# The last MoE phase of a fused attention and two-MoE kernel: the second MoE's first two token pairs woven into it, its last four output operands converted in place

## The chip, the cores and the metric

One NeuronCore of a Trainium2 chip runs the whole program. The metric is the device time of one execution in microseconds. The engines run side by side, each through its own queue in program order: TensorE (PE in the rows, with PEld for its weight loads), VectorE (DVE), ScalarE (ACT), GpSimd (POOL), and SyncE (SP), which issues most transfers.

## The reference

```python
out = softmax(q @ k.T / 8) @ v              # chunks of 64 positions, 8 heads, 4608 tokens
x   = (h := out @ w_in) * clip(h + 3, 0, 6) / 6 @ w_out      # first MoE, 512 -> 2048 -> 512
h   = x @ w_in2                              # second MoE, 512 -> 1024
s   = h * softmax(h)
out = ((s - mean(s)) / sqrt(var(s) + 1e-6) * g_ln) @ w_out2  # 1024 -> 512
```

All data are float32. The kernel keeps float32 precision by splitting each operand into a rounded high part and the low rest, and by adding up three of the four products.

## The kernel before, in words

Tokens are handled in 9 blocks of 512 in the first MoE. Blocks 3 to 8 are handled as three pairs of blocks. The function `pair` computes one pair in two phases. The **first phase** runs over 16 chunk pairs `j` and computes the hidden layer with seven block products per `j` (a Strassen-Winograd scheme), gates half of the results and parks the other half in DRAM (`held`). The **second phase** (steps `i` = 0 to 15) loads the parked results, gates them (ACT a relu, DVE a multiply), splits them (ACT a cast to `g_hi`, DVE a subtraction to `g_lo`) and multiplies them with `w_out`: one call of `moe_o` is 12 matmuls into the banks `acc`, and the call for step `i` stands on TensorE two steps later, before that step's other work. After the last call, the four `acc` banks are moved out (L548, L550) and stored to `x2d`.

The second MoE works on 18 pairs of 128-token tiles. For a pair `p`, `fetch_x2` loads its tokens, `combine_x2` forms four sums on DVE, `split_x2` makes the high parts on ACT and the low parts (`x_lo`). `product_1` to `product_7` are seven products of six matmuls each, into three banks `a`, `b` and `c`, of which `sum_2`, `sums_7`, `product_3` and `product_4` form the two hidden tiles on DVE. Each tile `t` then goes through `soft_1` (DVE row maximum, ACT exponential), `soft_2` (DVE), `turn` (DVE transposes inside blocks of 32, then block moves: by DMA from SP, by POOL in `pool_moves`, by ACT in `rest_moves`, eight copies), `chain_square` and `chain_rstd` (variance), `split_l` (the split for the last product), and `out_mm` (24 matmuls into a bank `po`). The main loop over `p` lays the work out so that the outputs on TensorE lag two pairs behind the products.

The weights of the second MoE are prepared while the last pair's first phase runs: the class `Second` reads them, forms the combined operands, splits them, and stores them to DRAM (`st2`); `load_2` brings them back in the second phase, when SBUF space has come free. `end_work(i)` is called at the end of each step `i` of the last second phase. It issues these loads and the preparation of pair 0, and from the table `EARLY` its products, in steps 11 to 15.

The order on every engine is the order of the code (`manual_schedule`); the pools only add the waits for buffers. A line that matters for what follows:

```python
        if at == NF - 1:
            for dc in range(KD):
                ...
                if dc % 2 == 0:
                    nc.scalar.mul(out=xo, in_=acc[dc], mul=1.0 / 6.0)
```

Of the kernel before, what the change touches and what calls it, by code (L numbers as in the profile page):

```python
# [16 lines left out]
P = 128  # L17
# [4 lines left out]
def tile_kernel(  # L22
# [168 lines left out]
    class Second:  # L191

        def __init__(self):
            w = wide("kbd")
            self.free = [w[:, i] for i in range(2)]
# [27 lines left out]
        def scale(self):  # L223
            if self.chunks and self.scaled != self.chunks[0]:
                self.scaled = self.chunks[0]
                r = self.raw[self.chunks[0]][:, :, 1]
                nc.scalar.activation(out=r, in_=r, func=AF.Copy, scale=2.0**-112)

# [37 lines left out]
        def step(self):  # L266
# [18 lines left out]
        def hi(self):  # L285
            for item in self.small:
                if len(self.halves) == 2 or not self.places:
                    break
                if item[0] == "lo" and item[1] in self.w and not self.ready(item):
                    i, w = self.places.pop(0), self.w[item[1]]  # L290
                    if i == 3:
                        t = [wcp.tile([P, DM], F32R, tag=f"{n}3", name=n) for n in ("s", "xo")]
                    else:
                        t = wide("pbd", F32R) if i == 2 else wi_slot(NF - 2 + i, F32R)
                        t = pair_of(t)
# [20 lines left out]
    LOADS = [n for n, (o, j) in enumerate(OPERANDS) if o[0] == "B" or o == "T1"]  # L316
    LOADS += [n for n in range(len(OPERANDS)) if n not in LOADS]

    def load_2(n):

        name, j = OPERANDS[n]
        homes = {"B11": 0, "T1": 1, "B21": 2, "B22": 3}
        if name == "out":
            t = wi[KD * NS + j] = wi_slot(KD * NS + j, F32R)
        elif name in homes:
            t = wi_slot(4 * j + homes[name], F32R)
            w2[name, j] = pair_of(t)
        elif j == 0 and name in ("T2", "T3"):
            t = wide({"T2": "kbd", "T3": "pbd"}[name], F32R)
            w2[name, j] = pair_of(t)  # L330
        else:
            t = None
            w2[name, j] = {
                ("T4", 0): lambda: (narrow(ap2, "v"), narrow(ap2, "v")),
                ("T2", 1): lambda: (narrow(ap2, "p"), narrow(ap2, "p")),
                ("T3", 1): lambda: (narrow(ap1, "q"), narrow(ap1, "tx0")),
                ("T4", 1): lambda: (narrow(ap1, "tx1"), narrow(ap1, "tx2")),
            }[name, j]()
        if t is None:
            for i in range(2):  # L340
                nc.sync.dma_start(out=w2[name, j][i].bitcast(F32), in_=st2[n][:, i])
        else:
            nc.sync.dma_start(out=t.bitcast(F32), in_=st2[n])
# [184 lines left out]
    def moe_o(b, f, g, at=None):  # L528
# [105 lines left out]
    def fetch_x2(p):  # L634
        if p < NU // 2:
            if p == 1:
                xr2[p] = [wo_slot(4 + i, F32).rearrange("p c (j t) -> p (c j) t", t=P) for i in range(2)]
            else:
                xr2[p] = [xrp.tile([P, 8, P], F32, tag=f"xr{i}", name=f"xr{i}") for i in range(2)]
# [55 lines left out]
    def bank(p, tag):  # L695

        if p:
            c_t[p, tag] = ps_2.tile([P, DM], F32, tag=tag, name=tag)
        else:
            if not early:  # L700
                early.append(att_psum())
            c_t[p, tag] = h_psum() if tag == "c" else early[0][:, int(tag == "b")]
        return c_t[p, tag]

    early = []

    def part(p, n):
        c_t[p, n] = work_tile("xo" if n == "s1" and not p else "s", name=n)
        return c_t[p, n]
# [66 lines left out]
    def turn(t):  # L776
# [3 lines left out]
        m = ring(8, 2, t).rearrange("p (b x) -> p b x", b=4)  # L780
# [48 lines left out]
    def l_tiles(i):  # L829

        if i < 3:
            return [
                (wo_slot(10 + 2 * i + k, F32R).rearrange("p c (f t) -> p (c f) t", t=P),)
# [41 lines left out]
    def out_mm(t):  # L875
# [3 lines left out]
        for a, ws in ((l_hi, (0, 1)), (l_lo, (0,))):  # L879
            for f in range(NF2):  # L880
                for w in ws:
                    nc.tensor.matmul(  # L882
                        po, a[f], wi[KD * NS + f][:, w],
# [232 lines left out]
    def pair(p, todo):  # L1116
# [6 lines left out]
        for j in range(NJ):  # L1123
# [37 lines left out]
            mul7(a, j, "A12", "B21", False, True)  # L1161
            if fill:
# [12 lines left out]
            mul7(c, j, "S4", "B22", False, True)  # L1175
            c12 = work_tile("xo")
# [42 lines left out]
        if final:  # L1219
            flush()  # L1220
            for n in LOADS[-3:]:
                load_2(n)
        return todo

    def end_work(i):
        m = len(OPERANDS) - NF2
        for n in LOADS[m * i // 11 : m * (i + 1) // 11] if i < 11 else LOADS[m + i - 11 :][:1]:
            load_2(n)
        if i == 0:
            fetch_x2(0)  # L1230
        elif i == 4:
            combine_x2(0)
        elif i == 5:
            split_x2_hi(0)
            split_x2_lo(0, 0, nc.vector)
        elif i == 6:
            split_x2_lo(0, 1, nc.vector)
            fetch_x2(2)
        elif i == 7:
            fetch_x2(1)  # L1240
        elif i == 9:
            combine_x2(1)
        elif i == 10:
            split_x2_hi(1)
            split_x2_lo(1, 0, nc.vector)
        elif i == 11:
            split_x2_lo(1, 1, nc.vector)
        for step in EARLY.get(i, ()):
            step(0)


    EARLY = {
        11: (product_1,),
        12: (product_6, product_2),
        13: (product_5, product_7, sums_7),
        14: (product_4,),
        15: (product_3,),
    }
# [85 lines left out]
    product_1(1)  # L1344
    soft_1(1)
    product_6(1)
    sum_2(1)
    combine_x2(2)
    split_x2(2)
    fetch_x2(3)  # L1350
    soft_1(0)
    product_2(1)
    product_7(1)
    product_5(1)
    sums_7(1)
    soft_2(1)
    turn(1)
    product_4(1)
    product_3(1)
    product_1(2)  # L1360
    product_6(2)
    sum_2(2)
    pool_moves(1)
    rest_moves(1)
    soft_2(0)
    product_2(2, False)
    product_7(2)
    product_5(2)
    chain_square(1)
    sums_7(2)  # L1370
    turn(0)
    split_l_hi(1)
    chain_square(0)
    keep_2(2)
    pool_moves(0)
    rest_moves(0)
    split_l_lo(1)
    soft_1(3)
    combine_x2(3)
    product_4(2)  # L1380
    product_3(2)
    split_l(0)
    split_x2(3)
    soft_1(2)
    chain_rstd(0)
    out_next()
    soft_2(3)
    fetch_x2(4)
    turn(3)
    square(3)  # L1390
    out_next()
    product_1(3)
    soft_1(5)
    soft_2(2)
    product_6(3)
    sum_2(3)
    turn(2)
    chain_square(2)
    split_l(3)
    stores()  # L1400
    pool_moves(2)
    rest_moves(2)
    combine_x2(4)
    soft_1(4)
    product_5(3)
    product_2(3)
    soft_2(5)
    split_x2(4)
    split_l(2)
    chain_rstd(1)  # L1410
    for p in range(3, NP):
        last = 2 * p - 2
        if p > 3:
            product_1(p)
            stores()
            split_l(last - 2)
            product_6(p)
            product_5(p)
            sum_2(p)
            turn(last + 1)  # L1420
            square(last + 1)
            product_2(p)
            soft_2(last)
            product_7(p)
# [102 lines left out]
```

## Time and profile before

| what | value |
|---|---|
| runs before | 1226.52, 1226.36, 1223.59 us; median 1226.36 us |
| the profiled execution | 1226.5 us, of which the span of the instructions is 1224.7 us |
| TensorE busy | 1190.7 us, 97% of the span |
| VectorE, ScalarE, GpSimd busy | 952.3, 656.9 and 381.8 us |
| mean granted TensorE clock | 0.993 |

TensorE's busy time is that of overlapping matmuls; a matmul of 512 columns shows some 390 ns, and a new one begins every 227 ns when nothing is in the way. Times in the trace count from the first instruction. The last second phase starts at 792.5 us, the second MoE's own part (after `es.close()`) at 852.5 us.

### The profile page before, as it was taken

The page shows a single profiled execution, that of the slowest core. Times are in us where ns is not written, and L with a number is a line of the kernel's source. Part 1 is how long each engine was busy: PE and PEld are TensorE (multiplying, and loading weights), DVE is VectorE, ACT ScalarE, POOL GpSimd, SP SyncE. Part 2 cuts the span into 40 slices and gives each one's busy share as a digit, 9 for nine tenths or more (in the row PEclk, how much of TensorE's full clock was granted, in tenths as well). Part 3 has the DMA queues.
Part 4 walks back from the last instruction along what each step waited for, and adds up shares of the span by engine and source line. Part 5 has one row for each costly group of instructions (what it writes and reads, how often), then busy time and mean ns, then how long its engine had stood idle before and what let it go on. Part 6 is the DMA issues. An engine that isn't in the chain of part 4 may idle for free.

```text
span 1224.7 us, 20699 instructions
## 1 busy us (share of the span) xinstructions
PE 1190.7 (97%) x7268; PEld 970.7 (79%) x7268; DVE 952.3 (78%) x1754; ACT 656.9 (54%) x1353; POOL 381.8 (31%) x466
## 2 busy tenths in 40 slices
PE   6899999999999999999999999999989999999998
PEld 5677788878788888888888888887768888888887
DVE  7999687787677779777778777774997878878774
ACT  4676455453322237322246343363788777877775
POOL 3000243530011110011100112100676767665865
PEclk9999999999999999999999999999999999999999
DMA  9800584441355537355445798794222323232311
GB/s 369 362 26 27 210 304 132 159 152 61 104 198 207 194 108 249 108 189 190 175 138 201 264 335 291 252 377 174 86 68 90 99 71 99 72 97 69 100 54 63
DMA packets 110360, 199.82 MB, mean 163 GB/s; under 512 B 14000, under 2 KB 49072, under 8 KB 107184
## 3 DMA queue, kind: packets, MB, share of 16 engines
q1 hardware_dynamic: 103920, 186.97, 44.1%
q10 hardware_dynamic: 6336, 11.54, 2.5%
q8 instruction: 57, 0.93, 0.3%
q14 instruction: 47, 0.39, 0.1%
HBM read 129.50 MB, written 58.20 MB: 153 GB/s over the span
## 4 chain that ended last, share of the span: by engine, by line
PE 83%; DVE 11%; ACT 2%; issue 1%; DMA 1%; SPq 1%; POOL 1%; DVEq 0%; ACTq 0%; POOLq 0%
PE acc L537 28%; PE po L882 14%; PE hp L1040 14%; PE hp L498 7%; PE att L1040 5%; PE b L684 5%; PE c L684 3%; PE a L684 3%; PE att L386 3%; DVE s L171 2%; DVE g_lo L523 1%; SPq L797 1%; DVE s L163 1%; DVE pbd L460 1%; PE att L684 1%
## 5 line engine op out<-in xcount | busy, mean ns | idle before, releaser
L537 PE MATMUL acc<-g_hi,wo 128*128 128x512 f32 x1152 | 294.9, 393 | 1.4 <-ACT g_hi L520 1.3
L537 PEld LDWEIGHTS acc<-g_hi,wo 128*128 128x128 f32 x1152 | 215.4, 189 | 48.8 <-DVE xo L550 1.9
L523 POOL TENSOR_TENSOR g_lo<-t,g_hi 128x512 fp32r<-128x512 f32 x45 | 65.6, 1457 | 450.8 <-ACT g_hi L520 450.8
L537 PE MATMUL acc<-g_lo,wo 128*128 128x512 f32 x576 | 160.0, 389 | 1.3 <-DVE g_lo L523 1.3
L882 PE MATMUL po<-wi,wo 128*128 128x512 f32 x648 | 152.5, 392 | 1.3 <-ACT ob L891 1.3
L882 PEld LDWEIGHTS po<-wi,wo 128*128 128x128 f32 x648 | 122.6, 189 | 27.5 <-ACT ob L891 1.7
L1040 PE MATMUL hp<-wi,ws 128*128 128x512 f32 x576 | 142.7, 390 | 0.0
L460 DVE STREAM_TRANSPOSE pbd<-p 32x128 f32<-32x128 f32 x448 | 135.5, 303 | 6.7
L537 PEld LDWEIGHTS acc<-g_lo,wo 128*128 128x128 f32 x576 | 108.2, 188 | 24.3 <-DVE g_lo L523 1.7
L1040 PEld LDWEIGHTS hp<-wi,ws 128*128 128x128 f32 x576 | 107.9, 188 | 23.7 <-DVE s L1146 1.2
L665 POOL TENSOR_TENSOR x_lo<-xr,x_hi 128x768 fp32r<-128x768 f32 (+1 forms) x32 | 70.3, 2218 | 135.0 <-DVE xr L651 64.0
L797 ACT COPY wo<-wo 32x256 f32<-32x256 f32 x228 | 92.0, 404 | 17.4 <-DVE wo L779 11.3
L498 PE MATMUL hp<-x_hi,wi 128*128 128x512 f32 x384 | 97.9, 397 | 2.0 <-ACT wi L352 1.9
L520 ACT CAST g_hi<-t 128x512 fp32r<-128x512 f32 x112 | 69.4, 620 | 53.0 <-DVE t L513 36.0
L498 PEld LDWEIGHTS hp<-x_hi,wi 128*128 128x128 f32 x384 | 72.5, 191 | 18.9 <-ACT wi L352 2.7
L1106 ACT ACTIVATE t<-att,three 128x512 f32<-128x512 f32 x24 | 16.5, 688 | 130.4 <-PE att L1040 113.8
L769 DVE SCALAR_TENSOR_TENSOR wo<-wo,r,wo 128x1024 f32<-128x1024 f32 x36 | 77.4, 2151 | 1.3
L1011 POOL TENSOR_TENSOR xo<-tx,xo 128x512 fp32r<-128x512 f32 x16 | 20.8, 1320 | 181.7 <-ACT xo L1005 167.0
L1040 PE MATMUL att<-wi,wa 128*128 128x512 f32 x288 | 73.1, 389 | 0.0
L866 POOL TENSOR_TENSOR wo<-wo,wo 128x1024 fp32r<-128x1024 f32 x26 | 63.4, 2439 | 6.8 <-ACT wo L862 3.3
L1040 PEld LDWEIGHTS att<-wi,wa 128*128 128x128 f32 x288 | 54.1, 188 | 11.3
L504 ACT ACTIVATE t<-hp,three 128x512 f32<-128x512 f32 x48 | 33.1, 691 | 50.4 <-PE hp L498 50.4
(269 smaller groups left out, 2194.6 us busy)
## 6 DMA issues: line engine op xcount, KB each, us to landing
ws<-sts SPq DMA_DIRECT2D x24, 1024.0 KB, 6.7
wa<-stw SPq DMA_DIRECT2D x24, 512.0 KB, 4.0
held<-xo SPq DMA_DIRECT2D x42, 256.0 KB, 2.2
s<-held SPq DMA_DIRECT2D x42, 256.0 KB, 4.4
wo<-wo SPq DMA_DIRECT2D x328, 32.0 KB, 1.8
x2d<-xo SPq DMA_DIRECT2D x36, 256.0 KB, 3.0
out<-ob SPq DMA_DIRECT2D x36, 256.0 KB, 2.2
v<-in_v SPq DMA_DIRECT2D x34, 256.0 KB, 2.7
```

Source lines behind the costliest of these rows:

```text
L460: nc.vector.transpose(out=pb[o : o + 32, s // 2, s % 2], in_=pv[s * 32 : s * 32 + 32, c, e],)
L498: nc.tensor.matmul(hp, wi[f][:, a, kk * P : (kk + 1) * P], b[:, kk], start=(n == 0), stop=(n == 3 * KD - 1),)
L520: nc.scalar.copy(out=g_hi, in_=t)
L523: eng.tensor_sub(out=g_lo, in0=t, in1=g_hi.bitcast(F32))
L537: nc.tensor.matmul(acc[dc], wo[f][:, w, dc * P : (dc + 1) * P], g[i], start=(at == 0 and n == 0), stop=(at == NF - 1 and n == 2),)
L665: eng.tensor_sub(out=lo[:, f], in0=r, in1=hi[:, f].bitcast(F32))
L684: nc.tensor.matmul(ps, x[:, AT[a], j], w2[w, j][i], start=(start and n == 0), stop=(stop and n == 5), skip_group_check=True,)
L769: nc.vector.scalar_tensor_tensor(out=h, in0=e, scalar=r, in1=h, op0=ALU.mult, op1=ALU.mult, accum_out=mu)
L797: move(out=m[b * 32 : b * 32 + 32, a], in_=tr[a * 32 : a * 32 + 32, b])
L866: eng.tensor_sub(out=lo, in0=m, in1=hi.bitcast(F32))
L882: nc.tensor.matmul(po, a[f], wi[KD * NS + f][:, w], start=(n == 0), stop=(n == 3 * NF2 - 1),)
L1040: nc.tensor.matmul(ps, w[:, i, kk * P : (kk + 1) * P], x[:, kk], start=(start and n == 0), stop=(stop and n == 5), skip_group_check=True,)
```

## The change

- Pairs 0 and 1 of the second MoE are both computed inside the steps of the last second phase: products of pair 0 in steps 3 to 8, those of pair 1 in steps 9 to 14, and between them the soft-max, the turning and the splits of their tiles as far as they are ready. The code after `es.close()` that did pairs 1 and 2 by hand is gone; the main loop begins at `p = 2`.
- `load_2` begins in the last chunk pair of the first phase (eight loads, and the first tokens of pair 0), and each operand takes the slots of the first phase's operand of the same name.
- The last four output operands are not stored to `st2` and loaded again: `place` gives them a home in SBUF, and `out_w` keeps them there. Four output operands are still loaded, in steps 9, 11, 13 and 15.
- Slots are renumbered (`ring(14, ...)`, `l_tiles`), pairs 0 and 1 share one PSUM tile for `a` and `b`, and the move of the `acc` banks goes ACT, ACT, DVE, DVE in place of turn about.

The core of the diff:

```diff
+        def place(self, kept):
+            if kept and all(any(t is w for t in self.free) for w in self.wide):
+                if len(self.free) > 2 or not self.chunks:
+                    self.free = [t for t in self.free if all(t is not w for w in self.wide)]
+                    self.wide = [None]
+                    return None, pair_of(wide("kbd", F32R))
...
+            i = min(self.places) if kept else max(self.places)
...
-                self.to_store.append((name, t, i))
+                if i is not None:
+                    self.to_store.append((name, t, i))
...
+                    kept = o == "out" and n >= LOADED_OUT
+                    i, t = self.place(kept)
...
+                    if kept:
+                        out_w[n] = t
...
+    LOADED_OUT = 4
+    out_w = {}
+    LOADS = [(n, j) for n in ("B11", "T2", "T1", "B21", "T3", "T4", "B22") for j in range(NS)]
+    LOADS += [("out", i) for i in range(LOADED_OUT)]
...
         else:
+            t = wi_slot(2 * XQ.index(o) + j, F32R)
+            w2[o, j] = pair_of(t)
+            nc.sync.dma_start(out=t.bitcast(F32), in_=st2[OPERANDS.index((o, j))])
...
-                if dc % 2 == 0:
+                if dc < 2:
                     nc.scalar.mul(out=xo, in_=acc[dc], mul=1.0 / 6.0)
...
-        if p:
+        if p > 1:
             c_t[p, tag] = ps_2.tile([P, DM], F32, tag=tag, name=tag)
         else:
+            if p not in early:
+                early[p] = att_psum()
+            c_t[p, tag] = h_psum() if tag == "c" else early[p][:, int(tag == "b")]
...
-        m = ring(8, 2, t).rearrange("p (b x) -> p b x", b=4)
+        m = ring(14, 2, t).rearrange("p (b x) -> p b x", b=4)
...
             mul7(a, j, "A12", "B21", False, True)
+            if final and lastj:
+                for n in range(4):
+                    load_2(n)
+                fetch_x2(0)
...
             mul7(c, j, "S4", "B22", False, True)
+            if final and lastj:
+                for n in range(4, 8):
+                    load_2(n)
...
     def end_work(i):
+        if 8 + i < len(LOADS) - LOADED_OUT:
+            load_2(8 + i)
+        elif i in (9, 11, 13, 15):
+            load_2(len(LOADS) - LOADED_OUT + (i - 9) // 2)
+        for step, *a in EARLY[i]:
+            step(*a)
...
+    EARLY = [
+        [],
+        [(combine_x2, 0)],
...
+        [(product_7, 1), (sums_7, 1), (turn, 1), (chain_square, 1)],
+        [(product_4, 1), (soft_2, 0), (split_x2_lo, 2, 0, nc.vector), (pool_moves, 1), (rest_moves, 1)],
...
-    product_1(1)
-    soft_1(1)
...
+    rest_moves(0)
     product_1(2)
+    chain_rstd(0)
     soft_1(2)
-    chain_rstd(0)
...
+    for p in range(2, NP):
...
+        if p == 2:
+            soft_2(3)
```

How it moves instructions is seen at three places. On TensorE, at the end of the last second phase, before (`acc` is a `moe_o` call, `hp` the last product of pair 0, `a` the first product of pair 1):

```order
L684 MATMUL hp<-wi_8299,x_lo 128x512
L537 MATMUL acc_8176<-g_hi,wo_1159 128x512 x2
L537 MATMUL acc_8177<-g_hi,wo_1159 128x512 x2
...
L537 MATMUL acc_8177<-g_hi,wo_1250 128x512 x2
L537 MATMUL acc_8177<-g_lo,wo_1250 128x512
L684 MATMUL a<-wi_8132,x_hi 128x512 x2
```

And of the change at the same place, where the `hp` row is the last product of pair 1 and `a`, `b` are the first products of pair 2:

```order
L689 MATMUL hp<-wi_8304,x_lo 128x512
L545 MATMUL acc_8188<-g_hi,wo_1105 128x512 x2
...
L545 MATMUL acc_8189<-g_hi,wo_1250 128x512 x2
L545 MATMUL acc_8189<-g_lo,wo_1250 128x512
L689 MATMUL a<-wi_8053,x_hi 128x512 x2
```

So 42 matmuls of pair 1 have moved from behind the phase into it, and three `moe_o` calls stand between them and pair 2. On VectorE, in the last steps of that phase, before (L513 is the gate, L523 `g_lo`, L742 to L753 are sums of pair 0, L550 the move out of `acc`, L758 the first row maximum of any tile):

```order
L513 SCALAR_TENSOR_TENSOR t<-t,s 128x512
L523 TENSOR_TENSOR g_lo<-t,g_hi 128x512
L748 TENSOR_TENSOR wo_8529<-s_8454,att 128x512
L523 TENSOR_TENSOR g_lo<-t,g_hi 128x512
L753 TENSOR_TENSOR wo_8491<-u_8483,hp 128x512
L550 TENSOR_SCALAR xo<-acc_8176 128x512
L550 TENSOR_SCALAR xo<-acc_8177 128x512
L758 TENSOR_REDUCE nmx<-wo_8529 128x1
```

And of the change, steps 13 to 15 (L753 and L758 are now the sums of pair 1's `product_4` and `product_3`, L771 to L778 `soft_2` of tile 0, L784 its `turn`, L871 the low part of `split_l` of tile 1, L521 and L531 the gate and `g_lo`):

```order
L753 TENSOR_TENSOR wo_8576<-s_8459,att 128x512
...
L774 SCALAR_TENSOR_TENSOR wo_8312,mu<-wo_8492,r,wo_8312 128x1024
L777 TENSOR_SCALAR mu<-mu 128x1
L778 TENSOR_SCALAR wo_8312<-wo_8312,mu 128x1024
L670 TENSOR_TENSOR x_lo<-xr_8418,x_hi 128x768
L521 SCALAR_TENSOR_TENSOR t<-t,s 128x512
L531 TENSOR_TENSOR g_lo<-t,g_hi 128x512
L758 TENSOR_TENSOR wo_8530<-u_8488,hp 128x512
L784 STREAM_TRANSPOSE wo_8663<-wo_8312 128x1024
L871 TENSOR_TENSOR wo_8671<-wo_8580,wo_8670 128x1024
L531 TENSOR_TENSOR g_lo<-t,g_hi 128x512
```

The gates and low parts that feed `moe_o` now stand behind whole rows of 1024 elements. On SP, at the end of the first phase, before (`held` are the parked results, `st` the stored operands, `x2d` the tokens):

```order
L1183 DMA held<-xo 128x512
L1112 DMA s<-held 128x512 x3
L343 DMA wi_8132<-st 128x1024
L644 DMA xr_8134<-x2d 128x4x128 x2
L551 DMA x2d<-xo 128x512 x4
```

And of the change:

```order
L1195 DMA held<-xo 128x512
L351 DMA wi_8053<-st 128x1024
...
L649 DMA xr_8061<-x2d 128x4x128 x2
...
L351 DMA wi_8105<-st 128x1024
L1117 DMA s<-held 128x512 x3
L351 DMA wi_8144<-st 128x1024
L559 DMA x2d<-xo 128x512 x4
```

Eight operand loads and the tokens now stand ahead of the first three loads of parked results.

## Rows read from the trace of the kernel before

**Rows 1.** The page: span, and busy time of each engine.

```profile
span 1224.7 us, 20699 instructions
PE 1190.7 (97%) x7268; PEld 970.7 (79%) x7268; DVE 952.3 (78%) x1754; ACT 656.9 (54%) x1353; POOL 381.8 (31%) x466
```

**Rows 2.** Stretches: PE, PEld, DVE, ACT, POOL busy (instructions); granted clock, DMA share, GB/s.

```profile
798.00:852.30 54.30, 53.49 (x235) 43.87 (x235) 30.65 (x49) 24.57 (x37) 0.00 (x0) 1.00 0.73 272
852.30:925.50 73.20, 67.37 (x277) 51.97 (x277) 67.97 (x100) 59.02 (x115) 45.95 (x63) 0.98 0.30 96
925.50:1220.80 295.30, 295.30 (x1304) 244.32 (x1302) 227.08 (x342) 219.98 (x405) 198.81 (x283) 1.00 0.26 80
...
920.00:925.50 5.50, 5.50 (x22) 4.47 (x21) 4.98 (x8) 5.33 (x14) 3.25 (x4) 0.83 0.21 61
...
800.00:835.00 35.00, 34.22 (x151) 27.99 (x150) 22.99 (x38) 19.66 (x29) 0.00 (x0) 1.00 1.04 387
```

**Rows 3.** Chain of waits that ended last: start, duration, what.

```profile
787.11 2.72 PE acc L537 x12
...
798.07 27.53 PE acc L537 x120
...
852.51 1.36 PE a L684 x6
...
925.75 1.36 PE b L684 x6
...
928.47 5.44 PE po L882 x24
...
1220.96 0.69 ACT ob L891
```

**Rows 4.** Timeline of TensorE: matmuls that waited longest after 852 us.

```profile
893.43 5.74 PE L882 MATMUL po<-wi,wo 128*128 128x512 f32 x24 [1.29 <-ACT ob L891]
...
917.05 0.73 PE L684 MATMUL b<-pbd,x_hi 128*128 128x512 f32 x2 [2.00 <-DVE u L723]
```

**Rows 5.** Timeline of VectorE: second phase, and one tile in the main loop.

```profile
807.28 0.42 DVE L649 TENSOR_TENSOR xr<-xr 128x256 f32<-128x256 f32 x1
...
808.74 0.68 DVE L513 SCALAR_TENSOR_TENSOR t<-t,s 128x512 f32<-128x512 f32 x1
809.39 0.69 DVE L523 TENSOR_TENSOR g_lo<-t,g_hi 128x512 fp32r<-128x512 f32 x1
810.00 0.95 DVE L665 TENSOR_TENSOR x_lo<-xr,x_hi 128x768 fp32r<-128x768 f32 x1
...
979.31 0.11 DVE L766 TENSOR_SCALAR r<-r 128x1 f32<-128x1 f32 x1
...
981.84 0.68 DVE L742 TENSOR_TENSOR u<-s,b 128x512 f32<-128x512 f32 x1
...
983.16 1.24 DVE L779 STREAM_TRANSPOSE wo<-wo 128x1024 f32<-128x1024 f32 x1
```

**Rows 6.** Lines L769 and L773 of `soft_2`: least, median and greatest duration, ns.

```profile
L769 DVE SCALAR_TENSOR_TENSOR wo<-wo,r,wo x36: 1284/2225/3422, 860.3 to 1201.1; 128x1024 f32<-128x1024 f32 x36
...
L773 DVE TENSOR_SCALAR wo<-wo,mu x36: 752/754/2579, 862.9 to 1204.1; 128x1024 f32<-128x1024 f32 x36
```

**Rows 7.** Groups after 852 us: busy us and mean ns, then idle before.

```profile
L758 DVE TENSOR_REDUCE nmx<-wo 128x1 f32<-128x1024 f32 x36 | 42.2, 1208 | 0.0
...
L797 ACT COPY wo<-wo 32x256 f32<-32x256 f32 x228 | 92.0, 404 | 17.4 <-DVE wo L779 11.3 <-DVE r L766 2.0 <-POOL g_lo L866 0.8
L761 ACT ACTIVATE wo<-wo,nmx 128x1024 f32<-128x1024 f32 x36 | 41.5, 1154 | 18.2 <-DVE nmx L758 18.1
...
L714 ACT COPY s<-a 128x512 f32<-128x512 f32 x17 | 10.0, 587 | 36.9 <-PE a L684 36.8
```

**Rows 8.** Loads of stored operands (L343), and the first relu on a parked result.

```profile
DMA to landing us min/median/max: 4.5/7.1/8.2
...
798.57 0.71 ACT L1106 ACTIVATE t<-s,three 128x512 f32<-128x512 f32 x1
```

More of the change, by code (lines that the diff above doesn't have):

```diff
@@ L194, in __init__ @@
             w = wide("kbd")
-            self.free = [w[:, i] for i in range(2)]
+            self.wide = [w[:, i] for i in range(2)]
+            self.free = list(self.wide)
             self.free.append(ap1.tile([P, DM], F32, tag="q", name="q"))
@@ L227, in scale @@
                 nc.scalar.activation(out=r, in_=r, func=AF.Copy, scale=2.0**-112)
+        def place(self, kept):
[4 more added lines that the diff above has]
+                    return None, pair_of(wide("kbd", F32R))
+            if not self.places:
+                return None, None
+            i = min(self.places) if kept else max(self.places)
+            if kept and i == 3:
+                return None, None
+            self.places.remove(i)
+            if i == 3:
+                return i, [wcp.tile([P, DM], F32R, tag=f"{n}3", name=n) for n in ("s", "xo")]
+            return None if kept else i, pair_of(wide("pbd", F32R) if i == 2 else wi_slot(NF - 2 + i, F32R))
         def words(self):
@@ L635, in fetch_x2 @@
         if p < NU // 2:
[L636 to L639, printed above, removed]
+            xr2[p] = [xrp.tile([P, 8, P], F32, tag=f"xr{i}", name=f"xr{i}") for i in range(2)]
             xr2[p] = [x.rearrange("p (n j) t -> p n j t", j=2) for x in xr2[p]]
@@ L1220, in pair @@
             flush()
-            for n in LOADS[-3:]:
-                load_2(n)
         return todo
     def end_work(i):
[L1226 to L1258, printed above, removed]
+        if 8 + i < len(LOADS) - LOADED_OUT:
[7 more added lines that the diff above has]
+        [(combine_x2, 0)],
+        [(split_x2_hi, 0), (split_x2_lo, 0, 0, nc.vector)],
+        [(split_x2_lo, 0, 1, nc.vector), (fetch_x2, 1), (product_1, 0)],
+        [(product_6, 0), (sum_2, 0)],
+        [(product_2, 0), (product_5, 0), (combine_x2, 1)],
+        [(product_7, 0), (sums_7, 0), (split_x2_hi, 1), (split_x2_lo, 1, 0, nc.vector)],
+        [(product_4, 0), (split_x2_lo, 1, 1, nc.vector)],
+        [(product_3, 0), (fetch_x2, 2)],
+        [(soft_1, 1), (product_1, 1)],
+        [(product_6, 1), (sum_2, 1), (soft_1, 0), (combine_x2, 2)],
+        [(product_2, 1), (product_5, 1), (soft_2, 1), (split_x2_hi, 2)],
+        [(product_7, 1), (sums_7, 1), (turn, 1), (chain_square, 1)],
+        [(product_4, 1), (soft_2, 0), (split_x2_lo, 2, 0, nc.vector), (pool_moves, 1), (rest_moves, 1)],
+        [(product_3, 1), (turn, 0), (split_l, 1, nc.vector), (chain_square, 0)],
+        [(soft_1, 3), (split_x2_lo, 2, 1, nc.vector), (pool_moves, 0), (fetch_x2, 3)],
+    ]
     pend = []
@@ L1368, in tile_kernel @@
[L1368 to L1383, printed above, removed]
-    soft_1(2)
-    chain_rstd(0)
[L1386 to L1411, printed above, removed]
+    rest_moves(0)
+    product_1(2)
+    chain_rstd(0)
+    soft_1(2)
+    for p in range(2, NP):
         last = 2 * p - 2
-        if p > 3:
+        if p > 2:
             product_1(p)
[L1415 to L1424, printed above, removed]
-            sums_7(p)
-            turn(last)
-        else:
-            turn(last + 1)
-            square(last + 1)
-            product_7(p)
-            sums_7(p)
-            soft_2(last)
-            turn(last)
-            fetch_x2(5)
+        stores()
+        split_l(last - 2)
+        product_6(p)
+        product_5(p)
+        sum_2(p)
+        if p == 2:
+            soft_2(3)
+        turn(last + 1)
+        square(last + 1)
+        product_2(p)
+        soft_2(last)
+        product_7(p)
+        sums_7(p)
+        turn(last)
@@ L1435, in tile_kernel @@
         out_next()
         square(last)
-        if p > 3:
-            next_x(p + 1)
+        next_x(p + 1)
         split_l(last + 1)
@@ L1442, in tile_kernel @@
         product_3(p)
-        if p > 3:
-            stores()
+        stores()
         out_next()
```

73 lines of the change are left out of this document (14 added, 59 removed).

## The prediction

> **What bounds the kernel now.** The page comes first: TensorE is busy 97% of the span, no other engine over 78% [rows 1]. So time can only come from the places where TensorE stands still, and these have to be found. The chain of waits gives the pace: 24 matmuls in 5.44 us, 0.2267 us each [rows 3]. From the first `moe_o` call of the last second phase (798.07) to the end of the last output (1220.96) the program has 16 calls of 12, 18 pairs of 42 and 36 output tiles of 24, that is 1812 matmuls, worth 410.7 us; the stretch took 422.9, so 12.2 us are lost in it. The chain says where. Until pair 1 begins (852.51) stand 234 matmuls, worth 53.0 in 54.4: 1.4 lost. From there to 925.75 stand 276 (pairs 1 and 2, then two outputs, pair 3 and two more outputs, mixed), worth 62.6 in 73.2: 10.7 lost. After that 1302, worth 295.1 in 295.2: nothing lost. The view of busy time by stretch shows the same: in 852 to 925 TensorE falls to 67 of 73 us while VectorE is at 68 of 73; afterwards TensorE has no gap at all and VectorE is at 77% [rows 2]. The timeline of TensorE says what ended the waits: an output bank not yet moved out, a sum on VectorE [rows 4]. These are the start of a pipeline: the first tile has to go through maximum, exponential, `soft_2`, turn, moves and split, and there is too little other matmul work to cover that. Meanwhile VectorE stands at 30.7 of 54.3 us and POOL at nothing in 798 to 852 [rows 2]. Part of the 10.7 is clock: 0.83 was granted in 920 to 925.5, between the levels of 1.2 and 2.4 GHz, right after the wait of 2.0 us at 915 to 917 [rows 2, 4].
>
> **The change part by part.** The matmuls stay the same in number; 42 of pair 1 (9.5 us) move into the second phase. Without a stall that phase then runs 798.07 + 16 x 2.72 + 14 x 1.36 = 860.6, with pair 0's products in 803 to 827, pair 1's in 829 to 852.5 and three `moe_o` calls behind them. The first outputs then lie 6.8 us and some 15 us behind 860.6, and the loop has its steady order from the start. So the whole 12.2 us can go, and what is left is what the woven phase and the first section of the loop newly wait for.
>
> VectorE in steps 9 to 15 is the first suspect. Counted from start to start, a gate is 0.65, a low part or sum of 512 columns 0.61, the four sums of `combine_x2` 1.46, `x_lo` 0.95 for 768 columns [rows 5], the maximum 1.21 [rows 7], the turn 1.24 and `soft_2` 2.53 with POOL at rest (979.31 to 981.84) [rows 5]. Each step has one gate and one low part (1.26). Step 10 (sum, maximum, four sums) makes 4.5, step 11 (`soft_2`) 3.8, step 12 (two sums, turn) 3.7, step 13 (sum, `soft_2`, `x_lo`) 5.4, step 14 (sum, turn, low part of `split_l`, by columns 1.27) 4.4: 21.8 against 21.8 us of matmuls in these steps. VectorE is as full as TensorE there, but what it makes is not due at once: the low part of step i is read by the call that stands two steps later, 4.1 us or more behind.
>
> The tightest point is therefore worked through. `product_4` of pair 1 ends at 848.4. From then VectorE runs without a break: sum 0.61, `soft_2` 2.53, `x_lo` 0.95, gate and low part 14 1.26, sum 0.61, turn 1.24, `split_l` 1.27, low part 15 0.61; that ends at 857.5. The call that reads it begins at 857.9 and needs it for its third matmul, 858.4. Cover 0.9 us; each hand-over between engines can eat some of it: 0 to 1.0 us of stall.
>
> Next ScalarE. The maximum of tile 3 ends at 858.7, its exponential (1.15 and 0.19 for the read-out, estimate 1.3) at 860.0, then two moves out of `acc` (0.59 each, by the copy of the same size) 861.2, then tile 0's eight `rest_moves` at 0.404 each, 864.4, then the copy `s1` of pair 2, 865.0 [rows 7]. `product_2` of pair 2 may overwrite nothing before that and is due at 860.6 + 3 x 1.36 = 864.7. Stall 0.3, with what comes late from VectorE up to 1.3.
>
> Third, `product_4` of pair 2, due at 873.2 behind the first output. VectorE: `u2` 865.6, `soft_2` of tile 3 868.1, turn 869.4, `soft_2` of tile 2 871.9, `u3` 872.5. Cover 0.7, if `soft_2` runs at its least. But now POOL works too (`split_l` of tile 0 from about 867), and the two large operations of `soft_2` range from 1.28 to 3.42 and from 0.75 to 2.58 [rows 6]. One blocked L773 makes it 1.1 late: 0 to 1.1.
>
> On that spread the Trainium skill ("SBUF — State Buffer", Who interferes with whom) says that VectorE and GpSimd share a port pair under an exclusive lock: a VectorE operation with two SBUF inputs or in a two-port mode waits out a GpSimd operation that reads SBUF. The rows agree: least in the trace where POOL rests, up to 2.1 us more elsewhere. By that rule the third point is late by 1.1 us or more, by the least durations not at all; I take the middle in the sum below.
>
> The other parts go together at nothing. The eight 256 KB stores and loads that the kept operands save, and the conversions in the first phase, lie beside matmuls that do not wait; VectorE's operations there are the same in number. The earlier loads relieve 800 to 835, where the DMA engines were full (share 1.04, 387 GB/s) [rows 2]; the wait there is part of the 1.4. The new order of moves out of `acc` (ACT, ACT, DVE, DVE) frees the first bank pair after two ScalarE copies of 0.59 in a row in place of 0.6 and 0.69 side by side, and banks come ready 0.68 apart: between -0.1 and +0.1 at each of six block ends.
>
> On SP, everything behind the eight early loads is later: the first three loads of parked results. The last two of the eight wait for the products with B21, which end at 787.1 [rows 3]; the first relu on a parked result ran at 798.6, and stored operands took 4.5 to 8.2 us to land [rows 8]. 787.1 + 1 of issue + 8.2 = 796.3: covered by 2 us, cost 0.
>
> Sum: -12.2, and +0.3 to +3.4 of new stalls, of which I take 2.0 (0.5, 0.7 and 0.8): -10.2 against the profiled execution's own 1226.5 us (span 1224.7 and 1.8 around it), which is 0.1 above the median of the runs: **1216 us**.
>
> **The rivals.**
> - A, as above: the start of the second MoE hides in the phase. For it: VectorE half idle there and POOL free. By the bounds of the stalls, -11.9 to -8.8, and 1.5 us for the spread of the runs, 1213 to 1219.
> - B, VectorE becomes the bound in steps 10 to 15: its 21.8 us of work leave nothing for the waits on products and on ScalarE's exponentials, which stand in the same queue as the relus. Each step of 4.1 us that loses 0.8 to 1.3 to such a wait pushes TensorE; over five or six steps and the first section of the loop, where POOL blocks `soft_2`, 4 to 8 us come back: 1219 to 1223. Against it: the calls lag two steps.
> - C, it does not do what it says: the start is only moved. The first section of the loop (tiles 2 and 3, maximum to split) is again without cover, and waits of 0.8 to 2.0 as in rows 4 return there for some 8 to 12 us: 1223 to 1227. Against it: two outputs of 5.44 us now stand in that section.
> - D, slower: SP. If the eight loads and the tokens (4.7 MB) landed one behind the other at 7.1 us, the first parked result would come after 840, not before 798, and TensorE would stand for 40 us: 1256. It decides from the point where the first parked result lands later than 798.6 + 10.2, where the gain is gone; every further microsecond costs one. Needed is a rate under some 250 GB/s from the first load (about 779) on; 387 were moved in 800 to 835 [rows 2].
>
> The Trainium skill ("TensorE: Matmul & The Clock Gate", What's actually happening) has the low clock as the default that activity lifts; B's waits could then cost clock too, as the one of 2.0 us did, which would put B at its upper end.
>
> **How the numbers follow.** A 0.62, B 0.22, C 0.10, D 0.06. The forecast is A's. The range takes A and nearly all of B: 1212.5 to 1222.5. About 0.3% (3.7 us) is what a measurement here can tell from no change, so faster means below 1222.7: A and nine tenths of B, 0.82; the rest of B and nearly all of C are the same, 0.12; D, 0.06.
>
> **What would show it.** In the trace after: the phase's last call ends at 861 to 863 and the whole part from there on takes 1536 matmuls' worth, 348.2 us, with 1 to 3 us more. Right for the first suspect: TensorE's waits behind 844 stay under 1 us each, and any is on `g_lo` of step 15. Right for the second and third: short waits of the products of pair 2 on the copy `s1` and on `u3`. B shows as TensorE waiting on sums or `g_lo` in several steps from 833 on; C as waits between 861 and 900 like those of rows 4; D as the relus waiting for loads at 797 to 805. The granted clock of 850 to 900 at 1.00 goes with A. The prediction fails most easily where I took least durations on a full VectorE: a few tenths in each of its waits add up, because after step 12 it has no idle time to catch up.

## The result and the profile after

The changed kernel ran in 1214.07 us (median of 6, 1212.95 to 1215.15) beside 1226.44 for the kernel before on the same chip: a ratio of 0.9901 with a 95% interval of 0.9887 to 0.9916, 12.1 us. Two later series gave 0.9908 and 0.9910. The profiled execution took 1213.9 us with a span of 1212.2, against 1224.7 [rows 1].

The page after has the span and the busy times:

```profile
span 1212.2 us, 20680 instructions
PE 1184.8 (98%) x7268; PEld 968.8 (80%) x7268; DVE 948.3 (78%) x1757; ACT 655.9 (54%) x1353; POOL 375.8 (31%) x463
```

The matmuls are as many as before; TensorE stands still less. The timeline of TensorE says where; these are the starts of the first `moe_o` call of the last second phase, of pair 2's first product, and of the last matmul (start, duration, what):

```profile
794.24 0.69 PE L545 MATMUL acc<-g_hi,wo 128*128 128x512 f32 x2
...
857.12 1.07 PE L689 MATMUL a<-wi,x_hi 128*128 128x512 f32 x4
...
1208.10 0.39 PE L887 MATMUL po<-kbd,g_lo 128*128 128x512 f32 x1
```

Before, the first of them stood at 798.07 [rows 3], and the last matmul started at 1220.49 (the last eight began at 1218.90, 0.2267 us apart). So the 12.5 us between the two spans have two parts. **3.8 us** lie ahead of the last second phase, in work that the new order of the second MoE does not touch. **8.5 us** lie in the part that the prediction speaks of: from the first `moe_o` call to the last matmul's start it took 422.4 us and now takes 413.9; 1811 matmuls of 0.2267 us are 410.5, so of 11.9 us lost 3.4 are left. (The prediction's 12.2 counts to the last move out, one matmul and 0.2 us later.) I call this length the stage below. In the three profiled executions of the changed kernel it repeats within 0.1 us, while whole times scatter by some 3 us.

The view of busy time by stretch (as rows 2) says where the 3.4 are: 0.3 up to 857.12 (276 matmuls are 62.6 us), 3.1 from there to 892.97, where TensorE falls to 33.7 of 35.9, nothing after that. The last line is the stretch in which the DMA engines were full before [rows 2]:

```profile
794.24:857.12 62.88, 62.88 (x278) 51.73 (x278) 48.59 (x77) 35.73 (x60) 6.59 (x12) 1.00 0.47 156
857.12:892.97 35.85, 33.69 (x146) 26.93 (x145) 30.40 (x46) 29.38 (x60) 18.86 (x31) 1.00 0.32 102
892.97:1208.50 315.53, 315.52 (x1392) 260.91 (x1391) 244.03 (x371) 236.75 (x437) 213.39 (x301) 1.00 0.26 81
800.00:835.00 35.00, 35.00 (x156) 28.94 (x155) 23.12 (x36) 16.06 (x26) 0.00 (x0) 1.00 0.60 200
```

Only two matmuls behind 848 us still wait for longer than 0.2 us by the timeline of TensorE (in brackets the wait and what ended it), in place of the list from which rows 4 come:

```profile
870.95 1.19 PE L689 MATMUL b<-wi,x_hi 128*128 128x512 f32 x4 [1.20 <-DVE u L747]
...
885.87 1.19 PE L689 MATMUL b<-wi,x_hi 128*128 128x512 f32 x4 [0.97 <-DVE u L728]
```

And this is where the 3.8 us between these two executions come from. Long before the last phase, at the end of a block of the first MoE, TensorE waited for ScalarE. The kernel before, timelines of ScalarE, VectorE and TensorE (two moves out of `acc`, two casts of weight sums, two moves, a waiting matmul):

```profile
229.91 1.09 ACT L548 ACTIVATE xo<-acc 128x512 f32<-128x512 f32 x2 [0.22 <-PE acc L537]
...
233.09 0.62 ACT L1005 CAST xo<-tx 128x512 fp32r<-128x512 f32 x1 [0.91 <-DMA x2d<-xo]
236.16 0.62 ACT L1005 CAST xo<-tx 128x512 fp32r<-128x512 f32 x1 [2.46 <-DMA x2d<-xo]
...
232.28 1.28 DVE L550 TENSOR_SCALAR xo<-acc 128x512 f32<-128x512 f32 x2
...
248.02 0.69 PE L386 MATMUL att<-kbd,q 64*64 64x64 f32 x32 [2.82 <-ACT p L426]
```

After, the same place:

```profile
233.82 1.14 ACT L1010 CAST xo<-tx 128x512 fp32r<-128x512 f32 x2 [1.26 <-DMA x2d<-xo]
...
246.19 0.69 PE L394 MATMUL att<-kbd,q 64*64 64x64 f32 x32 [0.61 <-DMA kbd<-in_k]
```

Before, the second cast waited 2.46 us for a staging tile `xo` (one of the buffers that a result is written to on its way to memory) until its store had landed, and the exponentials behind it on ScalarE made TensorE wait 2.82 us. The granted clock of 250 to 275 was 0.94 before and is 1.00 after: 1.5 us of clock (0.06 x 25) on top of the 2.2 us by which the wait is shorter. The view of busy time by stretch, before and after (the third number from the end is the granted clock):

```profile
250.00:275.00 25.00, 25.00 (x193) 20.21 (x191) 19.54 (x52) 14.48 (x52) 9.32 (x10) 0.94 0.35 114
```

```profile
250.00:275.00 25.00, 25.00 (x199) 20.32 (x198) 20.79 (x50) 14.59 (x52) 10.97 (x10) 1.00 0.43 137
```

The whole 3.8 us belong to this pair of executions. In two later executions of the changed kernel the same `moe_o` call began at 797.16 and 796.00, only 0.9 and 2.1 us ahead of the kernel before, in part because they had lost clock at another place, of which the last section speaks.

### The profile page after: what moved, and what is told of

The parts are those of the page before. It is cut to its first block, busy times and chain, and to the rows that moved or that the text cites. A ratio compares the mean times of both kernels' runs of the same rounds, so it can differ in the third digit from the quotient of the medians.

```text
span 1212.2 us, 20680 instructions
## 1 busy us (share of the span) xinstructions
PE 1184.8 (98%) x7268; PEld 968.8 (80%) x7268; DVE 948.3 (78%) x1757; ACT 655.9 (54%) x1353; POOL 375.8 (31%) x463
## 5 line engine op out<-in xcount | busy, mean ns | idle before, releaser
L531 POOL TENSOR_TENSOR g_lo<-t,g_hi 128x512 fp32r<-128x512 f32 x45 | 65.5, 1456 | 450.1 <-ACT g_hi L528 450.1
L670 POOL TENSOR_TENSOR x_lo<-xr,x_hi 128x768 fp32r<-128x768 f32 (+1 forms) x30 | 63.3, 2132 | 80.0 <-ACT x_hi L663 80.0
L774 DVE SCALAR_TENSOR_TENSOR wo<-wo,r,wo 128x1024 f32<-128x1024 f32 x36 | 68.7, 1909 | 1.3
L871 POOL TENSOR_TENSOR wo<-wo,wo 128x1024 fp32r<-128x1024 f32 x25 | 64.0, 2561 | 6.7 <-DMA x2d<-xo 3.6
L531 DVE TENSOR_TENSOR g_lo<-t,g_hi 128x512 fp32r<-128x512 f32 x67 | 46.6, 695 | 15.5 <-PE acc L545 13.2
L406 DVE TENSOR_REDUCE mx<-att 128x8 f32<-128x512 f32 x33 | 22.7, 688 | 42.5 <-ACT wi L491 42.5
```

The lines of the kernel that those rows point to most:

```text
L531: eng.tensor_sub(out=g_lo, in0=t, in1=g_hi.bitcast(F32))
L670: eng.tensor_sub(out=lo[:, f], in0=r, in1=hi[:, f].bitcast(F32))
L774: nc.vector.scalar_tensor_tensor(out=h, in0=e, scalar=r, in1=h, op0=ALU.mult, op1=ALU.mult, accum_out=mu)
L871: eng.tensor_sub(out=lo, in0=m, in1=hi.bitcast(F32))
```

## The experiments

All ratios are to the kernel before on the same chip. Against the changed kernel, `pair1_behind` and `evict_alone` differ clearly by the whole time and `loads_late` just so; for the others the intervals overlap, and the stage and the traces carry the reading.

| kernel | ratio, 95% interval | median, us | stage, us |
|---|---|---|---|
| before | | 1225.4 to 1228.0 | 422.4 |
| changed (result) | 0.9901, 0.9887 to 0.9916 | 1214.1 | 413.9 |
| changed, again (`after_again`, `after_third`) | 0.9908, 0.9889 to 0.9927; 0.9910, 0.9893 to 0.9926 | 1215.7; 1215.3 | 413.9; 413.9 |
| `evict_alone` | 0.9979, 0.9969 to 0.9989 | 1224.9 | 423.7 |
| `evict_back` | 0.9931, 0.9915 to 0.9948 | 1219.0 | 414.2 |
| `evict_ring` | 0.9920, 0.9905 to 0.9935 | 1216.1 | 414.3 |
| `pair1_behind` | 0.9971, 0.9958 to 0.9984 | 1223.7 | 422.0 |
| `soft2_first`, `soft2_again` | 0.9887, 0.9867 to 0.9907; 0.9892, 0.9874 to 0.9910 | 1213.0; 1211.8 | 411.6; 411.6 |
| `lo0_on_dve` | 0.9900, 0.9882 to 0.9918 | 1214.1 | 413.0 |
| `loads_late` | 0.9945, 0.9927 to 0.9963 | 1219.7 | 418.4 |
| `tokens_early` | 0.9939, 0.9921 to 0.9957 | 1218.1 | 416.5 |
| `stored8` | 0.9916, 0.9898 to 0.9935 | 1217.0 | 413.9 |

The changed kernel alone, run with two of the three later series:

> The changed kernel itself, unaltered, as the measure for the three beside it on the same chip. Every theory: 0.9901 of the kernel before, within 0.2%.

> The changed kernel again, as the measure on the same chip for the three beside it; every theory: 0.990 of the kernel before within 0.2%.

### The order of moves out of `acc`

One line alone, added to the kernel before and taken from the changed kernel:

```diff
-                if dc % 2 == 0:
+                if dc < 2:
```

> The kernel before with one line of the change alone: the first two of a block's four moves out of acc on ScalarE, the last two on VectorE. Theory 1: this line, which I costed at nothing, is what removed the wait of 2.82 us at 248 us and the lower clock behind it (0.94 in 250 to 275 us), so it alone gives 2 to 3.6 us: 1222.8 to 1224.4 against 1226.4, and the wait at 248 becomes one of some 0.6 us. Theory 2 (the forecast's own term): nothing, within 0.6 us, and the earlier start of the last second phase has another cause in the change.

> The changed kernel with that line put back (ScalarE and VectorE in turn). Theory 1: the wait at 248 us returns with its clock, 2 to 3.6 us longer than the changed kernel: 1216.1 to 1217.6, and the first moe_o call of the last second phase lies at 797 to 798 in place of 794.6. Theory 2: unchanged, 1214.1.

Theory 1 both times. The line alone gives 0.21% (2.6 us), and without it the changed kernel is 0.21 to 0.30% slower (2.6 to 3.7 us, against the changed kernel's ratios from its three other series; the intervals touch or overlap). The trace decides. The waits of TensorE at this place and the granted clock of 250 to 275 are 0.4 us and 1.00 with the line alone, and 3.0 us and 0.94 without it (waits of TensorE from 200 to 300 us in sum, number and longest, the stretch, and the first `moe_o` call of the last second phase; first `evict_alone`, then `evict_back`):

```profile
PE att L386 <- DMA kbd<-in_k: 0.4, 1, 0.4
...
250.00:275.00 25.00, 25.00 (x199) 20.30 (x198) 21.45 (x52) 14.04 (x49) 10.99 (x10) 1.00 0.44 147
...
795.01 0.69 PE L537 MATMUL acc<-g_hi,wo 128*128 128x512 f32 x2
```

```profile
PE att L394 <- ACT p L434: 3.0, 1, 3.0
...
250.00:275.00 25.00, 25.00 (x172) 20.13 (x171) 19.70 (x52) 13.87 (x51) 8.69 (x9) 0.94 0.33 110
...
798.65 0.73 PE L545 MATMUL acc<-g_hi,wo 128*128 128x512 f32 x2
```

All fourteen profiled executions of this document agree: in the two with the old order of moves (the kernel before and `evict_back`) this wait is 2.8 and 3.0 us and the clock 0.94, in the twelve others it is at most 1.0 us and the clock 1.00. In `evict_alone` the stage is 1.3 us longer than in the kernel before: a product of pair 1 now waits 1.64 us for a sum (L742), so the line gave back there a part of what it won.

What the line does, ScalarE first or tiles in turn, was told apart by leaving the engines to the banks as before and changing the order of the moves:

```diff
-            for dc in range(KD):
+            for dc in (0, 2, 1, 3):
                 xo = x_stage()
-                if dc < 2:
+                if dc % 2 == 0:
```

> The changed kernel with the moves out of acc in the order 0, 2, 1, 3: ScalarE still takes banks 0 and 2 and VectorE 1 and 3, as in the kernel before, but the staging tiles and SP's stores now come in the order in which the moves are made, ScalarE's two first. Theory 1: what cost the 2.82 us at 248 was the second staging tile, which stood behind VectorE's late move and its store, so that ScalarE's second cast of the sums waited; with the order of tiles mended the wait is gone and the time is the changed kernel's within 0.8 us. Theory 2: what counts is which engine frees which pair of banks; then the wait of 2.8 to 3.0 us and the clock return, 3 to 4 us slower than the changed kernel.

Both casts now run at once, as with the line, and the wait at 248 us is gone (timelines of ScalarE and TensorE):

```profile
233.80 1.14 ACT L1010 CAST xo<-tx 128x512 fp32r<-128x512 f32 x2 [1.27 <-DMA x2d<-xo]
...
246.19 0.69 PE L394 MATMUL att<-kbd,q 64*64 64x64 f32 x32 [0.65 <-ACT p L434]
```

So it was the second staging tile: in the order 0, 1, 2, 3 it belonged to VectorE, which came to its moves at 232.3, over 2 us after ScalarE's, and SP stores the tiles in order. Which engine frees which bank counts for little: ScalarE's second move at the end of the last phase waits 0.36 us for its bank, the eight `rest_moves` and `s1` of pair 2 are as much later, and `product_2` of pair 2 waits 0.41 us. That is the stage's 0.4 us more; by the ratio 1.2 us are given up in all, by the medians 0.8, both inside the intervals.

### Pair 1 out of the phase

The seven products and the sums of pair 1 and the row maximum of its tile 3 taken from the table `EARLY` (a step of it as an example; six more go the same way) and put behind the phase, with pair 1's products in the banks of the later pairs:

```diff
-        [(product_7, 1), (sums_7, 1), (turn, 1), (chain_square, 1)],
+        [(turn, 1), (chain_square, 1)],
...
+    for step in (product_1, product_6, product_5, sum_2, product_2, product_7, sums_7, product_4, product_3):
+        step(1)
+    soft_1(3)
```

> The changed kernel with pair 1's seven products, its soft_1 and soft_1(3) taken out of the woven phase and put in one piece behind it; turn, split and the loads stay where they are in the order, so that tile 1 and tile 0 pass through them as late as their data allow. Theory 1: the 42 matmuls of pair 1 inside the phase are cover for the first tiles' way through VectorE and ScalarE, and without them the waits of rows 4 return: 3 to 9 us slower, 1217 to 1223, with waits of TensorE of 1 us or more behind the phase. Theory 2 (rival C's view turned round): what helped is that the loads and pair 0 begin earlier, and where pair 1 stands makes no difference: within 1 us of 1214.1.

Theory 1, at its upper end: the stage is 422.0 us, as before the change, and the ratio is 0.0061 to 0.0070 above the changed kernel's, 7.5 to 8.6 us. The starts of the first `moe_o` call, of pair 1's first product and of the last matmul:

```profile
796.10 0.72 PE L545 MATMUL acc<-g_hi,wo 128*128 128x512 f32 x2
...
854.05 1.07 PE L689 MATMUL a<-wi,x_hi 128*128 128x512 f32 x4
...
1218.06 0.39 PE L887 MATMUL po<-kbd,g_lo 128*128 128x512 f32 x1
```

TensorE's longest waits by its timeline:

```profile
846.98 2.11 PE L545 MATMUL acc<-g_hi,wo 128*128 128x512 f32 x8 [1.47 <-ACT g_hi L528]
851.65 0.50 PE L545 MATMUL acc<-g_lo,wo 128*128 128x512 f32 x1 [1.21 <-DVE g_lo L531]
860.90 1.20 PE L689 MATMUL a<-wi,x_hi 128*128 128x512 f32 x4 [2.61 <-ACT s L719]
```

Of the 11.5 us lost 4.9 are lost inside the phase (796.10 to 854.05, 57.95 us for 234 matmuls): TensorE, 9.5 us of matmuls short, reaches the calls before their gates and splits are done. The rest comes where products and sums stand in one piece. The early loads and pair 0's earlier start are still in this kernel, and without pair 1 as cover they bring the stage nothing.

### The two waits that were left

`soft_2` of tile 3 ahead of `sum_2` of pair 2:

```diff
-        sum_2(p)
         if p == 2:
             soft_2(3)
+        sum_2(p)
```

> The changed kernel with soft_2 of tile 3 issued ahead of sum_2 of pair 2, so that it does not meet POOL's low part of split_l(0). Theory 1: VectorE's order behind the phase sets the two waits left (1.20 us at 871 on u of L747, 0.97 at 886 on u of L728), so both shrink to under 0.3 us and the kernel is 1.5 to 2.3 us faster: 1211.8 to 1212.6. Theory 2: ScalarE is what comes late there (s1 behind the eight rest_moves, the exponential of tile 5 at 879): VectorE waits as long, and the time stays within 0.6 us of 1214.1. Against both: u2 of pair 2 now lies behind soft_2, so product_2 or product_7 of pair 2 may wait up to 1 us in place of it, and the sum stays the same.

> The changed kernel with soft_2 of tile 3 ahead of sum_2 of pair 2, beside the changed kernel on one chip. Its trace had no wait of TensorE left behind the phase, and 348.7 us in place of 351.0 from pair 2's first product to the last matmul's start. If that is the order's doing, 1.7 to 2.5 us faster than the changed kernel; if it was one execution's luck, no difference (within 0.6 us).

The low part of `split_l` of tile 0 on VectorE in place of POOL:

```diff
-        split_l(last - 2)
+        if p == 2:
+            split_l_hi(0)
+        else:
+            split_l(last - 2)
...
         turn(last)
+        if p == 2:
+            split_l_lo(0, nc.vector)
```

> The changed kernel with the low part of split_l(0) on VectorE behind turn(2), so that POOL reads nothing from SBUF while VectorE runs soft_2 of tile 3. In the trace after, that soft_2's first operation took 2.71 us beside POOL's 2.41 us. Theory 1: POOL's operation is what holds VectorE's up; without it the operation falls to 1.3 to 1.5 us, u of L747 is over a microsecond earlier and the wait of 1.20 us at 871 is gone: about 1.2 us faster than the changed kernel, less what the added operation of 1.27 us on VectorE takes from the next wait (0.97 at 886): 0.2 to 1.2 faster. Theory 2: the long duration is the operation's own, for its operands: the wait stays, and with the added work it is 0 to 1.3 us slower.

The changed kernel, timelines of VectorE and POOL behind the phase (`sum_2` waiting for `s1`; the first `soft_2`'s last operation; POOL's low part):

```profile
861.27 0.69 DVE L728 TENSOR_TENSOR u<-s,b 128x512 f32<-128x512 f32 x1 [1.54 <-ACT s L719]
...
863.77 2.71 DVE L778 TENSOR_SCALAR wo<-wo,mu 128x1024 f32<-128x1024 f32 x1
...
863.52 2.41 POOL L871 TENSOR_TENSOR wo<-wo,wo 128x1024 fp32r<-128x1024 f32 x1 [3.56 <-DMA x2d<-xo]
```

The same operation of `soft_2` in `lo0_on_dve`, where POOL does not have that low part:

```profile
866.73 0.75 DVE L778 TENSOR_SCALAR wo<-wo,mu 128x1024 f32<-128x1024 f32 x1
```

It falls from 2.71 to 0.75 us, the wait of 1.20 us is gone, the other of 0.97 stays with 0.3 of a new one, and the stage is 0.9 us shorter. So POOL's operation held VectorE's up (theory 1; the stage's 0.9 lie within its 0.2 to 1.2, and the ratio shows no difference beyond its interval). The expectation names the operation as the first of `soft_2`; it is the last of the two large ones, and its duration without POOL is 0.75, not 1.3 to 1.5.

In `soft2_first`, VectorE does `soft_2` in the 1.54 us in which it waited for `s1`, and the next tile's `soft_2` meets POOL where nobody waits:

```profile
860.26 0.75 DVE L778 TENSOR_SCALAR wo<-wo,mu 128x1024 f32<-128x1024 f32 x1
...
863.03 2.71 DVE L774 SCALAR_TENSOR_TENSOR wo<-wo,r,wo 128x1024 f32<-128x1024 f32 x1
...
862.26 2.40 POOL L871 TENSOR_TENSOR wo<-wo,wo 128x1024 fp32r<-128x1024 f32 x1 [3.57 <-DMA x2d<-xo]
```

(These are of `soft2_again`.) No matmul of the stage waits for longer than 0.2 us; the stage is 411.6 us twice (in `soft2_again` from 792.93 to 1204.53), 2.3 less than the changed kernel's, with 1.1 left of the 11.9. Theory 1. It is the fastest version: by the ratios 0.14 to 0.18% ahead of the changed kernel. Their intervals overlap, so it is the stage that settles it.

### The early loads

The eight loads and the tokens issued behind the first phase, and then with the tokens early again:

```diff
             mul7(a, j, "A12", "B21", False, True)
             if final and lastj:
-                for n in range(4):
-                    load_2(n)
                 fetch_x2(0)
...
+        if final:
+            for n in range(8):
+                load_2(n)
```

(This is `tokens_early`; in `loads_late` the tokens move too, behind the fourth load.)

> The changed kernel with the eight loads and the fetch of the first tokens issued behind the last first phase (at the start of the second), in place of two points inside the first phase. Theory 1: the early issue is what lets pair 0 begin in step 3; issued later, the eight loads of 512 KB and the tokens queue with the parked results, product_1(0) stands behind step 3 waiting for its operands, and TensorE, which takes its work in order, waits: 3 to 8 us slower than the changed kernel. Theory 2: at 387 GB/s, the rate of 800 to 835 in the kernel before, the first 1 MB for step 3 needs 2.7 us and there are some 8 until then, so only the relus on parked results are at stake: 0 to 1 us slower.

> The changed kernel with the eight operand loads behind the first phase, as in the run with all of them late, but the tokens of pair 0 fetched early, as in the changed kernel. Theory 1: what was late there were the tokens (1.20 us on x_lo, 0.33 on x_hi), so most of the 4.5 us lost in the phase comes back: 0 to 1.5 us slower than the changed kernel. Theory 2: the loads stand ahead of the parked results on SP, and the relus that wait 3.4 and 2.1 us for them are what delays TensorE, in whatever place it then shows; then 3 to 4.5 us slower than the changed kernel.

`loads_late` lost 4.5 us of the stage, all ahead of pair 2: theory 1's size, but not quite its way. With the tokens early, 2.6 us of it stay, and 0.29% (3.6 us) by the ratio: between the two theories, nearer to the second. The 1.9 us that come back were the tokens' (waits of 1.20 us on `x_lo` and 0.33 on `x_hi`). The rest in `tokens_early` by the timelines of ScalarE and TensorE (a relu on a parked result, the copy `s1` of pair 0, and the product that waits for it):

```profile
802.09 0.72 ACT L1111 ACTIVATE t<-s,three 128x512 f32<-128x512 f32 x1 [3.17 <-DMA s<-held]
...
805.22 0.59 ACT L719 COPY s<-att 128x512 f32<-128x512 f32 x1 [1.90 <-DMA x2d<-xo]
...
805.85 1.20 PE L689 MATMUL att<-wi,x_hi 128*128 128x512 f32 x4 [2.58 <-ACT s L719]
```

Behind the operands, the parked results and the stores of `x2d` come late; they hold up ScalarE's relu and the copy, and TensorE pays at the product that needs the copy.

### All eight output operands stored

```diff
-    LOADED_OUT = 4
+    LOADED_OUT = 8
```

(with four more loads, in steps 6, 8, 10 and 12)

> The changed kernel with all eight output operands stored and loaded again; the four that it keeps go through memory as in the kernel before, and come back in steps 6, 8, 10 and 12 of the phase. Theory 1 (my term of 0): stores and loads lie beside matmuls that do not wait, so the time is that of the changed kernel within 1 us. Theory 2: the four operands kept in place save transfers of 2 MB that lie where the DMA queue is on the path: 1 to 3 us slower.

The stage does not change. But ScalarE issues those stores, and just ahead of the last calls of the first phase it stands behind them (timelines of ScalarE and TensorE):

```profile
787.81 0.69 ACT L1115 ACTIVATE t<-att,three 128x512 f32<-128x512 f32 x1 [2.68 <-DMA st<-s]
...
794.03 0.73 PE L549 MATMUL acc<-g_hi,wo 128*128 128x512 f32 x2 [1.09 <-ACT g_hi L532]
```

The changed kernel has no such wait. By the ratios the stores cost 0.08 to 0.15%, 1.0 to 1.8 us: the lower end of theory 2, from a queue that I had not looked at. The intervals overlap, so only the wait of 1.09 us is shown. The kernel before, which stored all eight too, had no such wait of TensorE from 600 us to its last phase: keeping four in place took no wait off it, and avoids one that `stored8` shows in the new order.

## Why the prediction was right, and where it was not

The forecast of 1216.0 us was 1.9 us above the result, inside its range. The place of the gain was right, but that the sum came so close is in part luck: two of its terms were off, with opposite signs. The stage gave 8.5 us in place of 10.2, and a term taken at 0 gave the rest.

- **The gain, -12.2 + 2.0 = -10.2.** The mechanism held: the start of the second MoE hides in the phase. `pair1_behind` shows that 0.4 us of the gain are left without pair 1's 42 matmuls in the phase, `loads_late` that about half of it also hangs on the early loads. The stage gained 8.5: the losses that were left came to 3.4, not 2.0. (The phase's last call ended at 857.1, not at the 861 to 863 given as a sign, because the whole phase lay 3.8 us earlier.)
- **Full VectorE in steps 9 to 15** (rival B). Refuted. VectorE ran without a break from 845.1 to 856 as worked out, the last `g_lo` ended at 854.06, 0.8 us ahead of the matmul that reads it (0.9 worked out), and no call of the phase waited for it: 0 for the 0.5. The phase lost 0.3 us in all. The two rows (VectorE, TensorE):

```profile
853.18 0.88 DVE L531 TENSOR_TENSOR g_lo<-t,g_hi 128x512 fp32r<-128x512 f32 x1
...
854.85 0.39 PE L545 MATMUL acc<-g_lo,wo 128*128 128x512 f32 x1
```

- **`product_2` of pair 2 on `s1`.** It started some 0.1 us late for the 0.7 taken; the maximum and the exponential of tile 3 came as worked out.
- **`product_4` of pair 2 on `u3`.** 1.20 us, against 0 to 1.1 with 0.8 taken. By the trace and `lo0_on_dve` the cause is POOL's low part beside `soft_2`. The Trainium skill's rule ("SBUF — State Buffer", Who interferes with whom: whichever engine issues first keeps the shared pair for its whole instruction) agrees: POOL began at 863.52 and VectorE at 863.77, POOL ended at 865.93 and VectorE 0.55 us later; 2.71 beside POOL, 0.75 without. (The place at 979.31 that the prediction takes for "POOL at rest" had POOL at work, but only on operations of 128x2.)
- **Not foreseen:** 0.97 us on `u2` of pair 3 (886 us). I had stopped working through VectorE at tile 2. The next tile's `soft_2` waits 3.0 us for an exponential and meets POOL again. `soft2_first` removes this wait too: that `soft_2` still meets POOL (2.58 to 2.60 us), but `u2` of pair 3 starts 2.3 us earlier in the stage and TensorE comes only 1.4 us earlier.
- **The order of moves out of `acc`, taken as 0 from -0.1 to +0.1.** This step failed. I looked at when banks come free, and not at the staging tiles that the moves write and that ScalarE's next work needs. It measured 2.6 us alone and 2.6 to 3.7 in the changed kernel (3.8 between the two profiled executions, clock included).
- **Loads and SP at 0** (rival D). Right: the first relu on a parked result ran at 794.02 without a wait. `loads_late` shows that this holds because they are issued early; the loads and the tokens issued some 14 us later (789.7 on SP, not 774.8, with the phase 0.9 us later too) cost 4.5 us, 1.9 of them the tokens' (`tokens_early`) and the rest largely by the way that D describes. D's 250 GB/s is the rate at which the first parked result begins to be late (5.0 MB from 779 to 798.6); for its own condition, 10.2 us later, the same sum gives some 170.
- **Kept operands at 0.** Right against the kernel before; in the changed kernel their stores would have made a call wait 1.09 us on ScalarE's queue.
- **C**, that the start only moves: refuted by the 8.5 us of the stage, with two short waits left behind the phase in place of 8 to 12 us.

## What to carry to other kernels

Matmuls of independent work moved into a phase are worth what they cover there: put them where the first tiles' long way through the other engines runs, and work VectorE's order through until the waits have died away, not only to the seam. When the engine of a move is changed, follow the buffer that it writes as well as the bank that it frees: with staging tiles and stores in turn, the slowest mover sets the pace for whoever needs the next tile. Compare stages by the trace when a per mille counts; they repeat far better than whole times.

## What the hardware showed that I had not expected

The same wait costs clock in one execution and none in another. At 147 to 149 us TensorE waits 2.2 to 2.3 us in every execution; behind it, 150 to 155 us, the granted clock in two executions of the changed kernel (the first of the result, the second of `after_again`) was

```profile
150.00:155.00 5.00, 5.00 (x23) 4.13 (x22) 4.81 (x12) 1.69 (x10) 2.24 (x4) 1.00 1.03 387
```

```profile
150.00:155.00 5.00, 5.00 (x35) 4.00 (x29) 4.20 (x10) 2.37 (x10) 3.29 (x5) 0.69 1.01 394
```

0.69 lies between the two levels of 1.2 and 2.4 GHz, and 0.31 x 5 is 1.5 us. Over 140 to 160 us the clock was 1.00 in eight of the fourteen profiled executions and 0.91 in the six others. A wait of 2.6 us at 331 us was followed by 0.83 over 330 to 340 in the first of the two and by 1.00 in `soft2_again`. At the start of the last second phase the two executions above lie 2.9 us apart: 1.2 of them arose before 134 us, 1.6 between the wait at 148 and the one at 246 to 249. Such places are a good part of the scatter of some 3 us between executions of one kernel; whether they are all of it is not shown. The Trainium skill ("TensorE: Matmul & The Clock Gate", What's actually happening) has the low clock as the default that activity lifts; that fits the fall behind a wait, and no run here shows what decides whether it comes.
